# Clustered attention and two feed-forward layers in one kernel: a start with one centroid load and fewer dummy transposes, and another order of moves, masks and splits ahead of the second and third pair of heads

## The chip, the cores and the metric

The kernel runs on one core of a Trainium2 chip as one launch. The metric is device time in microseconds (us). The engines are TensorE (PE; its weight loads have a row of their own, PEld), VectorE (DVE), ScalarE (ACT), GpSimd (POOL) and SyncE (SP), which here only issues DMAs.

## The reference

Inputs: q, k and v of shape (2, 8, 768, 64), 16 centroids for each of 8 heads, and the weights of two feed-forward layers, all float32.

```python
q_assign = argmax(normalise(q) . normalise(centroids))   # k_assign likewise
mask = q_assign[:, :, :, None] == k_assign[:, :, None, :]
scores = where(mask, q k^T / 8, -1e9)
x = softmax(scores) v                                    # as (1536, 512)
x = ((x @ w1) * (x @ w2)) @ w3 @ w_out
out = (sigmoid(x @ w_gate) * (x @ w_val)) @ w_out2
```

## The kernel before, in words

Attention comes first and lasts about 235 us. The 16 heads are worked in 8 pairs (`pr`), a pair's two heads (`e`) lying on partitions 0 to 63 and 64 to 127. A head has three blocks of 256 queries, so there are 48 blocks; block `i` belongs to pair `i // 6` and is its block `at = i % 6`. Every float32 operand is split into a high and a low part in fp32r.

A block's scores are two products for each tile of 128 queries (line 332): KH with QH, and KX with QX. KH holds k's high part in rows 0 to 63 and the mask of the clusters in rows 64 to 79, QH likewise for q; QX holds q's high part and, in rows 64 to 127, q's low part; KX holds k's. The rows are brought together by DMAs within SBUF: `move` (line 62) puts one on SP's queue. `prep_scatter(pr, e)` issues the six moves of a head's operands; `prep_mask(pr, e)` issues the four small moves of its one-hot clusters out of `ohT`, which VectorE turns (line 275) and of which POOL rescales the key half (line 294). For the head (1, 0), `prep_scatter` leaves out the move of q's low part; the kernel does it later by hand.

After the scores come the row maximum (DVE, line 344), the exponential (ACT, line 355), transposes of the exponentials through PE (line 365), their split into `ph` and `pl`, and the products with v (`weighted_v`, lines 406 and 407). The split is done by ACT and DVE, except for the first third of certain blocks (`by_pool`): there ACT copies to the single buffer `pc`, and POOL makes `ph` (line 54) and `pl` (line 59).

A pair's result is joined and normalised while the next pair runs: `join_x` moves, `add_x` (POOL, line 459), `spread` (two DMAs that broadcast the reciprocal sums into `r`, line 454), `norm_x` (POOL, line 463, which needs `r`), and `split_x` (POOL, two instructions).

The order on every engine is written out by hand: the loop over blocks calls these steps one after another, and each engine and each queue takes its instructions in that order. In block 7 (pair 1, `at == 1`) the loop calls `load_v(2)` and `prep_scatter(2, 1)`; in block 9 (`at == 3`) `prep_mask(2, 0)` and `prep_mask(2, 1)`, then `add_x(0)` and `spread(0)`; in block 11 `norm_x(0)` and `split_x(0)` on POOL; in block 12 the splits `ph` and `pl` on POOL, which PE uses in block 13.

Two side chains run along. `prep_split_1_lo` is a generator with three steps for the second pair: k's low part (POOL, line 208), a scaled copy of q (ACT, line 210), and q's low part (POOL, line 212). `f64_steps` turns a weight matrix from words of 64 bits into high and low parts in seven steps; the table `CONVERT` gives the block (pair, `at`) in which each of the later six is called; the last one is the split of the matrix on POOL.

At the start, `warm` issues dummy transposes on PE. The centroids are loaded into both halves of `c2` by two DMAs, then normalised, transposed by PE (line 520) and copied to `cw` (line 533); `prep_sims` multiplies q and k of pair 0 with them (line 241).

After attention the two feed-forward layers run as products of 128 x 512 tiles, with weights split in time by a list of due times. The change does not touch them.

Of the kernel before, what the change touches and what calls it, by code (L numbers as in the profile page):

```python
# [12 lines left out]
ALU = mybir.AluOpType  # L13
# [14 lines left out]
def tile_cluster_attention__then__moe__then__gated_moe(  # L28
# [15 lines left out]
    nc = tc.nc  # L44
# [16 lines left out]
    def move(dst, src):  # L61
        nc.sync.dma_start(dst.bitcast(F32), src.bitcast(F32))
# [70 lines left out]
    def warm(n, name):  # L133

        pt = ps_t.tile([128, 2, 256], F32, tag="t", name=name)
        for i in range(n):
            nc.tensor.transpose(pt[:, 0, 0:128], ident, ident)

    warm(17, "warm0")

    manual = ExitStack()
    manual.enter_context(tc.manual_schedule(engines={mybir.EngineType.PE, mybir.EngineType.DVE, mybir.EngineType.Activation, mybir.EngineType.Pool, mybir.EngineType.SP}))
# [5 lines left out]

    early = core.tile([128, S], F32, tag="xb", name="early", bufs=1)
    c2 = early[:, 0 : 2 * D].rearrange("p (j d) -> p j d", j=2)  # L150
    sq, nrm = early[:, 128:192], early[:, 192:196]
    for j in range(2):
        nc.sync.dma_start(c2[:, j, :], centroids.rearrange("h c d -> (h c) d"))
    cw = cent.tile([128, NP, 2 * C], F32, name="cw")
    nc.gpsimd.memset(cw, 0.0)
    dec = cent.tile([128, C], F32, name="dec")
# [64 lines left out]
    def prep_scatter(pr, e):  # L221
        qh, ql, kh, kl = opnd[pr, "hl"]
        r = slice(64 * e, 64 * e + 64)
        QH, KH, QX, KX = operands(pr, e)
        move(QH[0:64], qh[r])
        move(KH[0:64], kh[r])
        move(QX[0:64], qh[r])
        move(KX[64:128], kh[r])
        move(KX[0:64], kl[r])
        if (pr, e) != (1, 0):  # L230
            move(QX[64:128], ql[r])

    HALF = S // 2

# [43 lines left out]
    def prep_mask(pr, e):  # L278
        ohT = opnd[pr, "oh"]
        QH, KH, _, _ = opnd[pr, e]  # L280
        halves = [slice(HALF * h, HALF * h + HALF) for h in range(2)]
        if pr == 0 and e == 0:
            for h in range(2):
                nc.vector.tensor_scalar(out=KH[64:96, halves[h]], in0=ohT[64 + 32 * h : 96 + 32 * h], scalar1=-1.0, scalar2=BIG, op0=ALU.add, op1=ALU.mult)
                nc.scalar.copy(QH[64:96, halves[h]], ohT[32 * h : 32 * h + 32])
            return
        if pr == 0:
            for h in range(2):
                nc.scalar.activation(KH[64:96, halves[h]], ohT[64 + 32 * h : 96 + 32 * h], AF.Copy, scale=BIG, bias=-BIG)
            nc.scalar.copy(QH[64:96, halves[0]], ohT[0:32])  # L290
            move(QH[64:96, halves[1]], ohT[32:64])
            return
        if e == 0:
            nc.gpsimd.tensor_scalar(out=ohT[64:128], in0=ohT[64:128], scalar1=-1.0, scalar2=BIG, op0=ALU.add, op1=ALU.mult)
        for h in range(2):
            at = 32 * h + C * e
            move(QH[64 : 64 + C, halves[h]], ohT[at : at + C])
            move(KH[64 : 64 + C, halves[h]], ohT[64 + at : 64 + at + C])
# [207 lines left out]

    load_v(0, 0)
    convert(0)
    nc.vector.tensor_tensor(out=sq, in0=c2[:, 0, :], in1=c2[:, 0, :], op=ALU.mult)
    nc.vector.tensor_reduce(out=nrm[:, 0:1], in_=sq, axis=AX.X, op=ALU.add)  # L510
    nc.vector.tensor_scalar(out=nrm[:, 0:1], in0=nrm[:, 0:1], scalar1=1e-30, scalar2=None, op0=ALU.max)
    nc.scalar.activation(nrm[:, 1:2], nrm[:, 0:1], AF.Sqrt)
# [2 lines left out]
    nc.vector.tensor_tensor(out=nrm[:, 2:3], in0=nrm[:, 2:3], in1=nrm[:, 1:2], op=ALU.add)  # L515
    nc.vector.tensor_scalar(out=nrm[:, 2:3], in0=nrm[:, 2:3], scalar1=0.5, scalar2=1e-6, op0=ALU.mult, op1=ALU.add)
    nc.vector.reciprocal(nrm[:, 3:4], nrm[:, 2:3])
    nc.vector.tensor_scalar(out=c2, in0=c2, scalar1=nrm[:, 3:4], scalar2=None, op0=ALU.mult)
    cps = ps_a.tile([128, 128], F32, tag="a", name="cps")
    nc.tensor.transpose(cps, c2.rearrange("p j d -> p (j d)"), ident)  # L520
    warm(5, "warm1")
# [42 lines left out]
    words["av"], words["room"] = both[:, 0:256], both[:, 256:512]  # L564
    CONVERT = {}
    for n, slots in enumerate((
        ((0, 3), (0, 3), (0, 5), (1, 0), (1, 0), (1, 2)),
        ((6, 5), (7, 0), (7, 1), (7, 2), (7, 3), (7, 4)),
    )):
        for slot in slots:  # L570
            CONVERT.setdefault(slot, []).append(n)
    if True:
        for i in range(-2, NB + 2):
            pr, at = divmod(i, 6)
            nxt = pr + 1 if 0 <= i and pr + 1 < NPR else None
            later = nxt + 1 if nxt and nxt + 1 < NPR else None

            scores(2 * i + 3)
            if i == -1:
                warm(11, "warm3")  # L580
            split_hi(i - 1, 2)
            transposes(i, 0)
            if i == NB - 1:
                turn_sums(pr, ps_s.tile([128, 1024], F32, tag="s", name=f"rp{pr}")[:, 0:128])
            maxima(2 * i + 3)
            if i == 0:
                prep_code(0, 1)
                prep_onehot(0, 1)
                prep_turn(0, 1)
                prep_sims(1)  # L590
                prep_sum(1)
            if i == NB - 1:
                store_sums(pr)
            if later and at == 0 and pr:
                load_qk(later)
            if at == 0 and 0 < pr and i < NB:
                join_x(pr - 1, 0)
            if at == 1 and 0 < pr and i < NB:
                join_x(pr - 1, 1)
            if nxt and nxt > 1 and at == 1:  # L600
                load_v(nxt)
                prep_scatter(nxt, 1)
            if nxt and at == 3:
                for e in range(2):
                    if nxt == e == 1:
                        next(split_1_lo, None)
                        move(opnd[1, 0][2][64:128], opnd[1, "hl"][1][0:64])
                        prep_scatter(1, 1)
                    prep_mask(nxt, e)
            split_lo(i - 1, 2)  # L610
            split_hi(i, 0)
            split_lo(i, 0)
            if i == 0:
                prep_v(0, 1)
            if nxt and at == 1:
                prep_argmax(nxt)
            if nxt and at == 2:
                prep_onehot(nxt)
            if 0 < pr and i < NB and at == 5:
                norm_x(pr - 1)  # L620
                split_x(pr - 1)
            if nxt == 1 and at == 2:
                load_v(nxt)
            if 0 < pr and i < NB and at == 3:
                add_x(pr - 1)
                spread(pr - 1, "xb", 1)
            exponentials(2 * i + 3)
            if i == -1:
                next(split_1_lo)
                prep_argmax(0, 1)  # L630
                load_qk(2)
            if 0 <= i < NB and at == 4:
                guard_sums(pr)
            if later and at == 3:
                halves = prep_split(later)
                next(halves)
            if later and at == 4:
                for _ in halves:
                    pass
            weighted_v(i - 1, 0)  # L640
            weighted_v(i - 1, 1)
            if i == 1:
                prep_scatter(1, 0)
            if later and at == 5:
                prep_scatter(later, 0)
            loads = ((6, 4), (7, 1), (7, 3))
            if (pr, at) in loads:
                convert(1 + loads.index((pr, at)))

            similar = later if at == 5 else None  # L650
            if similar:
                prep_sims(similar)
            scores(2 * i + 4)
            turning = 0 <= i < NB - 1 and at == 5
            if turning:
                turn_sums(pr, sps[2 * i + 4][:, S : S + 128])
            if nxt and at == 1:
                prep_code(nxt)
            if 0 < pr < NPR and at == 0:
                prep_v(pr, 1)  # L660
            if nxt and at == 3:
                prep_v(nxt, 0)
            transposes(i, 1)
            split_hi(i, 1)
            weighted_v(i - 1, 2)
            transposes(i, 2)
            if i == NB:
                convert(2)
            take_x(i - 1)
            if i == NB:  # L670
                convert(3)
            if i == 0:
                prep_mask(0, 1)
            if similar:
                prep_sum(similar)
            maxima(2 * i + 4)
            if turning:
                store_sums(pr)
            if nxt and at == 2:
                prep_turn(nxt)  # L680
            if i == NB - 2:
                invert(pr)
            for n in CONVERT.get((pr, at), ()):
                convert(n)
            split_lo(i, 1)
            exponentials(2 * i + 4)
            if 0 <= i < NB - 2 and at == 4:
                invert(pr)
            if i == NB - 2:
                end_move(0)  # L690
            if i == NB:
                end_move(1, FIRST)
                spread(END, "raw", 4)
                end_add(0)
        end_move(1, LAST)
        end_add(1, FIRST)
        end_norm(FIRST)
        end_split(FIRST)
        end_add(1, LAST)
        end_norm(LAST)  # L700
        end_split(LAST)
# [551 lines left out]
```

## Time and profile before

| what | value |
|---|---|
| median of 3 runs | 754.03 us (751.93 to 754.36) |
| the profiled execution | 751.83 us |
| its span, first to last instruction | 749.7 us |
| PE busy | 741.2 us (99%) |
| DVE, ACT, POOL busy | 575.3, 473.2, 415.1 us |
| granted clock of PE, mean | 1.00 |

A row of the timeline reads: start in us from the span's start, duration in us, engine, source line, operation, tile written, tile read, count; in brackets the idle time of the engine just before and what ended it. SPq rows are the issues of DMAs on SP; the duration is that of the issue, not of the transfer. A row with a count above one stands for several instructions in a row.

### The profile page before, as it was taken

The numbers are of one execution on the slowest core, as the hardware profiler recorded it, in microseconds if no ns is written. First come the engines' busy times: TensorE is split into PE (matmuls) and PEld (weight loads), VectorE is DVE, ScalarE is ACT, GpSimd is POOL, SyncE is SP. The second block draws the span as 40 slices with busy tenths as digits, with TensorE's granted clock in tenths as the row PEclk, the third lists the DMA queues.
The fourth block names the chain that finished last, engine by engine and source line by source line (L and its number), as shares of the span: only waits on it lengthen the run. The fifth ranks groups of instructions, "written<-read, shape, count | busy, mean of one in ns | idle before, by whom it ended". The sixth has DMA issues, their size and how long they took to land.

```text
span 749.7 us, 12300 instructions
## 1 busy us (share of the span) xinstructions
PE 741.2 (99%) x4272; PEld 670.9 (89%) x4272; DVE 575.3 (77%) x893; ACT 473.2 (63%) x994; POOL 415.1 (55%) x420
## 2 busy tenths in 40 slices
PE   8999999999999999999999999999999999999998
PEld 6888988999998788888888999999999999999996
DVE  7999999999986677676743386685686968869675
ACT  7988888988985565555532365777757454565630
POOL 4768788878782655424321037775647645375510
PEclk9999999999999999999999999999999999999999
DMA  6687677685542543443430001221303113030004
GB/s 187 168 191 176 170 202 179 166 196 137 144 120 64 159 147 115 143 136 113 142 111 1 1 20 37 86 85 57 114 0 114 56 57 113 28 113 29 30 0 169
DMA packets 29198, 80.14 MB, mean 107 GB/s; under 512 B 5200, under 2 KB 6800, under 8 KB 29136
## 3 DMA queue, kind: packets, MB, share of 16 engines
q1 hardware_dynamic: 29136, 79.35, 36.5%
q8 instruction: 34, 0.56, 0.3%
q14 instruction: 28, 0.23, 0.1%
HBM read 52.49 MB, written 3.19 MB: 74 GB/s over the span
## 4 chain that ended last, share of the span: by engine, by line
PE 88%; DVE 3%; DMA 2%; POOL 2%; ACT 2%; issue 1%; SPq 1%; DVEq 0%; ACTq 0%; POOLq 0%
PE p L67 12%; PE p L66 12%; PE p L65 12%; PE s L332 7%; PE pt L365 7%; PE p_a L66 4%; PE p_a L67 4%; PE p_a L65 4%; PE av L406 4%; PE av L407 4%; PE p_b L65 2%; PE p_b L66 2%; PE p_b L67 2%; PE w34p L65 2%; PE w34p L66 2%; PE w34p L67 2%
## 5 line engine op out<-in xcount | busy, mean ns | idle before, releaser
L344 DVE TENSOR_REDUCE nm<-s 128x1 f32<-128x768 f32 x96 | 90.7, 947 | 8.3 <-PE s L332 7.2
L355 ACT ACTIVATE e<-s,nm 128x768 f32<-128x768 f32 x96 | 88.2, 919 | 11.6 <-DVE nm L344 11.2
L365 PE MATMUL pt<-ident,e 128*128 128x128 f32 x576 | 86.0, 273 | 0.2 <-DVE sm L248 0.2
L406 PE MATMUL av<-ph,vx 128*128 128x256 f32 x288 | 81.1, 309 | 0.1
L67 PE MATMUL p<-x,w 128*128 128x512 f32 (+1 forms) x208 | 80.3, 386 | 0.2 <-POOL w L120 0.2
L66 PE MATMUL p<-x,w 128*128 128x512 f32 (+1 forms) x208 | 80.1, 385 | 0.0
L65 PE MATMUL p<-x,w 128*128 128x512 f32 (+1 forms) x208 | 80.1, 385 | 0.0
L394 DVE TENSOR_TENSOR pl<-pt,ph 128x512 fp32r<-128x512 f32 x113 | 75.7, 682 | 5.0 <-ACT ph L383 3.7
L407 PE MATMUL av<-pl,vx 128*128 128x256 f32 x288 | 74.7, 287 | 0.6 <-DVE pl L394 0.2
L116 POOL TENSOR_TENSOR w_a<-w_f 128x512 uint32<-128x512 uint32 x30 | 32.1, 1070 | 77.2 <-DVE w_f L115 37.1
L383 ACT CAST ph<-pt 128x512 fp32r<-128x512 f32 x113 | 64.7, 590 | 15.0 <-PE pt L365 13.8
L365 PEld LDWEIGHTS pt<-ident,e 128*128 128x128 f32 x576 | 67.7, 141 | 4.5 <-DVE sm L248 0.5
L1132 DVE TENSOR_TENSOR acc<-p,acc 128x512 f32<-128x512 f32 x59 | 40.5, 687 | 29.3 <-PE p L67 29.2
L948 POOL TENSOR_TENSOR wgv_a<-wgv_f 128x512 uint32<-128x512 uint32 x24 | 25.3, 1053 | 66.7 <-DVE wgv_f L947 38.4
L1026 ACT COPY s<-p_a 128x384 f32<-128x384 f32 x72 | 34.5, 479 | 43.2 <-PE p_a L67 42.8
L407 PEld LDWEIGHTS av<-pl,vx 128*128 128x128 f32 x288 | 54.7, 190 | 3.1 <-DVE pl L394 3.0
L67 PE MATMUL p<-wo,u 128*128 128x512 f32 (+1 forms) x146 | 57.3, 393 | 0.0
L66 PE MATMUL p<-wo,u 128*128 128x512 f32 (+1 forms) x146 | 57.1, 391 | 0.0
L332 PE MATMUL s<-KH,QH 80*128 80x512 f32 x192 | 54.6, 366 | 2.4 <-DMA KH<-ohT_None 0.8
L65 PE MATMUL p<-wo,u 128*128 128x512 f32 (+1 forms) x146 | 56.3, 386 | 0.0
L406 PEld LDWEIGHTS av<-ph,vx 128*128 128x128 f32 x288 | 54.5, 189 | 1.8 <-ACT xa L415 0.6
L332 PE MATMUL s<-KX,QX 128*128 128x512 f32 x192 | 49.7, 340 | 0.3 <-DMA QX<-x 0.3
(254 smaller groups left out, 2223.2 us busy)
## 6 DMA issues: line engine op xcount, KB each, us to landing
wgv_f<-in_w_gv_dram SPq DMA_DIRECT2D x24, 512.0 KB, 3.3
wo_f<-in_w_out_dram SPq DMA_DIRECT2D x20, 512.0 KB, 3.2
w_f<-in_w_dram SPq DMA_DIRECT2D x16, 512.0 KB, 3.3
w_f<-in_w3T_dram SPq DMA_DIRECT2D x16, 512.0 KB, 3.3
raw<-in_qkT_dram SPq DMA_DIRECT2D x16, 384.0 KB, 4.5
r<-r_dram SPq DMA_DIRECT2D x16, 192.0 KB, 4.0
xb<-xa SPq DMA_DIRECT2D x15, 192.0 KB, 3.7
out_dram<-acc SPq DMA_DIRECT2D x11, 256.0 KB, 2.0
```

The costliest lines, as they stand in the source:

```text
L65: nc.tensor.matmul(ps, whi, xhi, start=start, stop=False, skip_group_check=more)
L66: nc.tensor.matmul(ps, whi, xlo, start=False, stop=False, skip_group_check=more)
L67: nc.tensor.matmul(ps, wlo, xhi, start=False, stop=stop, skip_group_check=more)
L332: nc.tensor.matmul(sp[:, c], products[n][0], products[n][1][:, c], start=n == 0, stop=n == 1)
L344: nc.vector.tensor_reduce(out=nms[j], in_=sps[j][:, 0:S], axis=AX.X, op=ALU.max, negate=True)
L355: nc.scalar.activation(et, sps.pop(j)[:, 0:S], AF.Exp, bias=nms.pop(j), accum_out=acc_x[pr, "sum"][:, at : at + 1])
L365: nc.tensor.transpose(pt[:, kk, 128 * t : 128 * t + 128], exps[2 * i + t][:, k0 : k0 + 128], ident)
L383: nc.scalar.copy(ph, pt)
L394: nc.vector.tensor_tensor(out=pl, in0=src, in1=ph, op=ALU.subtract)
L406: nc.tensor.matmul(avs[i], w, ph[:, kk, :], start=kt == 0, stop=False)
L407: nc.tensor.matmul(avs[i], w, pl[:, kk, :], start=False, stop=kt == KT - 1)
L1132: nc.vector.tensor_tensor(out=acc[:, t, :], in0=bk, in1=acc[:, t, :], op=ALU.add)
```

## The change

- `warm0` issues 15 dummy transposes in place of 17.
- The centroids are loaded once, into a tile `c1`; the scaling that writes `c2` reads `c1` twice by a broadcast view.
- `prep_scatter` issues all six moves for every head. The third step of `prep_split_1_lo` is called in block 0, ahead of `prep_v(0, 1)`; the separate move of q's low part in block 3 goes.
- `prep_scatter(2, 1)` goes from block 7 to block 9, between `prep_mask(2, 0)` and `prep_mask(2, 1)`.
- The last step of the first weight matrix goes from block (1, 2) to block (1, 1).

```diff
-    warm(17, "warm0")
+    warm(15, "warm0")
...
-    sq, nrm = early[:, 128:192], early[:, 192:196]
-    for j in range(2):
-        nc.sync.dma_start(c2[:, j, :], centroids.rearrange("h c d -> (h c) d"))
+    sq, nrm, c1 = early[:, 128:192], early[:, 192:196], early[:, 200 : 200 + D]
+    nc.sync.dma_start(c1, centroids.rearrange("h c d -> (h c) d"))
...
-        if (pr, e) != (1, 0):
-            move(QX[64:128], ql[r])
+        move(QX[64:128], ql[r])
...
-    nc.vector.tensor_tensor(out=sq, in0=c2[:, 0, :], in1=c2[:, 0, :], op=ALU.mult)
+    nc.vector.tensor_tensor(out=sq, in0=c1, in1=c1, op=ALU.mult)
...
-    nc.vector.tensor_scalar(out=c2, in0=c2, scalar1=nrm[:, 3:4], scalar2=None, op0=ALU.mult)
+    nc.vector.tensor_scalar(out=c2, in0=c1.unsqueeze(1).broadcast_to([128, 2, D]), scalar1=nrm[:, 3:4], scalar2=None, op0=ALU.mult)
...
-        ((0, 3), (0, 3), (0, 5), (1, 0), (1, 0), (1, 2)),
+        ((0, 3), (0, 3), (0, 5), (1, 0), (1, 0), (1, 1)),
...
                 load_v(nxt)
-                prep_scatter(nxt, 1)
+                if nxt > 2:
+                    prep_scatter(nxt, 1)
             if nxt and at == 3:
                 for e in range(2):
                     if nxt == e == 1:
-                        next(split_1_lo, None)
-                        move(opnd[1, 0][2][64:128], opnd[1, "hl"][1][0:64])
                         prep_scatter(1, 1)
                     prep_mask(nxt, e)
+                    if nxt == 2 and e == 0:
+                        prep_scatter(2, 1)
...
             if i == 0:
+                next(split_1_lo, None)
                 prep_v(0, 1)
```

## Rows read from the trace of the kernel before

**Rows 1.** The page's busy times: us, share of the span, instructions

```profile
PE 741.2 (99%) x4272; PEld 670.9 (89%) x4272; DVE 575.3 (77%) x893; ACT 473.2 (63%) x994; POOL 415.1 (55%) x420
```

**Rows 2.** PE's waits: line, releaser, us in total, times, longest

```profile
PE s L332 <- DMA KH<-ohT_None: 0.8, 1, 0.8
...
PE s L332 <- DVE KH L284: 0.6, 1, 0.6
PE s L332 <- DMA QX<-x: 0.3, 1, 0.3
```

**Rows 3.** Timeline of the start, all engines

```profile
0.74 0.86 SPq L153 DMA_DIRECT2D early<-in_centroids_dram  x2
...
4.38 0.29 DVE L518 TENSOR_SCALAR early<-early 128x128 f32<-128x128 f32 x1
...
5.64 0.46 DVE L533 COPY cw<-cps 64x64 f32<-64x64 f32 x2 [0.97 <-PE cps L520]
...
6.41 0.83 ACT L529 CAST KH<-raw 64x768 fp32r<-64x768 f32 x1 [0.37 <-DMA raw<-in_qkT_dram]
```

**Rows 4.** Stretches, dummies' loads: length, PEld busy (count), granted clock, DMA share, GB/s

```profile
1.51:4.99 3.48, 3.48 (x17) 1.00 0.70 202
7.19:10.23 3.04, 3.04 (x28) 1.00 0.76 299
```

**Rows 5.** Timeline of POOL and PE's loads, blocks 0 to 3

```profile
21.45 1.02 POOL L59 TENSOR_TENSOR vx<-vraw,vx 128x384 fp32r<-128x384 f32 x1
24.02 0.62 POOL L54 TENSOR_SCALAR ph<-pc 128x512 fp32r<-128x512 f32 x1 [1.54 <-ACT pc L380]
26.41 0.19 PEld L407 LDWEIGHTS av<-pl,vx 128*128 128x128 f32 x1
31.52 1.85 POOL L212 TENSOR_TENSOR x<-q,x 128x768 fp32r<-128x768 f32 x1
```

**Rows 6.** Timeline of blocks 7 to 10, the third pair's moves

```profile
55.52 0.46 SPq L62 DMA_DIRECT2D QH<-hi  x1
...
56.20 0.62 POOL L54 TENSOR_SCALAR ph<-pc 128x512 fp32r<-128x512 f32 x1 [1.86 <-PE s L332]
...
58.18 0.57 DVE L275 STREAM_TRANSPOSE ohT_None<-oh 128x384 f32<-128x384 f32 x1
...
60.39 0.83 SPq L62 DMA_DIRECT2D QH<-ohT_None  x1
...
62.85 0.58 SPq L62 DMA_DIRECT2D KH<-ohT_None  x1
...
64.94 0.59 PE L332 MATMUL s<-KH,QH 80*128 80x512 f32 x2 [0.79 <-DMA KH<-ohT_None]
...
66.06 1.18 SPq L454 DMA_DIRECT2D r<-r_dram  x2
```

**Rows 7.** One stretch, the weight tile on POOL: length, POOL busy (count), clock, DMA

```profile
58.50:60.60 2.10, 1.90 (x2) 1.00 0.98 222
```

**Rows 8.** Timeline of blocks 11 to 13, POOL and PE's loads

```profile
70.45 1.85 POOL L463 TENSOR_TENSOR xa<-xa,r 128x768 f32<-128x768 f32 x1 [1.41 <-DMA r<-r_dram]
...
75.82 1.27 POOL L59 TENSOR_TENSOR pl<-pc,ph 128x512 fp32r<-128x512 f32 x1
...
77.61 0.19 PEld L407 LDWEIGHTS av<-pl,vx 128*128 128x128 f32 x1
```

**Rows 9.** The tile r over the whole span: from issue to landing

```profile
DMA to landing us min/median/max: 3.7/4.0/4.8
```

**Rows 10.** Timeline of SP's queue, second pair's masks and moves

```profile
30.80 0.54 SPq L62 DMA_DIRECT2D QH<-ohT_None  x1
...
33.40 0.50 SPq L62 DMA_DIRECT2D QX<-x  x1
...
38.99 0.87 SPq L62 DMA_DIRECT2D QH<-ohT_None  x1
...
42.19 0.53 SPq L62 DMA_DIRECT2D QH<-hi  x1
```

## The prediction

> **What bounds the kernel now.** I read the page's busy times first, then TensorE's waits, then the timeline of the places where it waits. TensorE (PE) is busy for 741.2 of 749.7 us [rows 1]: time can only come out of its few idle stretches, and any new one is added in full. Its list of waits names three that the change touches [rows 2]: 0.8 us for a mask move into KH, 0.6 us for the first mask (DVE, line 284), 0.3 us for a move into QX. In the timeline the reader then looks, for each, at what stands just ahead of the late instruction on its own queue, and who is next in that queue.
>
> **Start: one centroid load, two dummies fewer.** The two centroid loads take 0.86 us of issue on SP, 0.43 us each [rows 3]; with one gone everything SP issues afterwards, the q and k of the first pair first, is issued 0.43 us sooner. ScalarE's KH waits for k at 6.41 [rows 3], so that should become 5.98. The normalised centroids are ready at 4.38 + 0.29 = 4.67 (then 4.24), but VectorE idles 0.97 us until 5.64 for their transpose [rows 3], which stands behind the 17 dummies; their weight loads fill 3.48 us up to 4.99 [rows 4], 0.205 us each. Two fewer let the transpose start 0.41 us sooner, at 4.58, still after the centroids. Similarities need both: they move by 0.41 us, and the chain on VectorE behind them leads to the mask for which PE waits [rows 2]. The broadcast operand in the scaling of the centroids I cost at nothing: the same 128x128 output, whose 0.29 us would hide in the 0.34 us between 4.24 and 4.58. I take -0.4; the bounds are -0.43 (the whole issue) and 0 (k lands no sooner because earlier transfers do not speed up its bytes).
>
> The loads of the dummies went from 0.205 us to 3.04 / 28 = 0.109 us each between the two stretches, the 1.2 and the 2.4 GHz level by their ratio of 1.9, although the granted clock in the record reads 1.00 in both [rows 4]; nearly everything that PE did until then was transposes. The Trainium skill, page "TensorE: Matmul & The Clock Gate", section "Part 4: PE-mode transpose", says that a transpose does not count as PE work in the same way and that full rate does not engage for it. By that rule dropping two dummies could not touch the clock, and the sum stays at -0.4; by the rows, dummies do raise it, so that fewer of them could raise it later. That is a rival below.
>
> **Second pair: q's low part.** POOL's 1.85 us subtraction at line 212 moves from 31.52 into block 0, ahead of the v split that ended at 21.45 + 1.02 = 22.47 [rows 5]. Behind that split POOL idled 1.54 us until 24.02 for `pc` [rows 5]; 1.85 us more is 0.3 us too many, and the low product of block 1 comes 0.3 us late. PE loads exactly that at 26.41 [rows 5], so I price +0.3 (0 to +0.35). In return the last QX move of this head no longer stands behind the subtraction: it joins the other five at block 1, many us before its use, and the 0.3 us wait goes [rows 2]. SP issues as many moves as before; the second head's six move up by one issue, and nobody waits for them. Net 0, from -0.3 to +0.35.
>
> **Weight split a block sooner.** Its two instructions, 1.90 us, now lie between 58.5 and 60.6 on POOL [rows 7], between `ohT_None`, ready at 58.18 + 0.57 = 58.75 [rows 6], and line 294, which two of the four mask moves need. One block sooner it falls into POOL's 1.86 us of idle time ahead of 56.20 [rows 6]. So nearly all of it is covered: at worst 0.1 us sticks out ahead of block 8. Nothing, by itself; it lets line 294 run at 58.75.
>
> **Third pair: masks first.** Now SP issues six moves of the second head from 55.52, then, from 60.39, eight mask moves, then at 66.06 the two loads of the reciprocal sums `r` [rows 6]. PE needs the first head's masks at 64.15 and gets them at 64.94, from the fourth mask move, issued at 62.85 [rows 6]: 0.79 us lost. After the change the order is four masks, six moves, four masks, `r`. The masks can start at 58.75; four of them took 2.6 us in the second pair (30.80 to 33.40) [rows 10], so the fourth is issued about 60.7, 2.1 us sooner. The 0.79 us goes.
>
> What is late next is `r`. The same 14 issues stand ahead of it, but the train starts at 58.75 and not at 55.52; SP has nothing to do in between. The train took 66.06 - 55.52 = 10.54 us [rows 6]; so `r` is issued at 69.3, 3.2 us later. The second pair has the new order already, with one issue more: 30.80 to 42.19 [rows 10], 11.39 us for 15, or 10.6 for 14. Now POOL is the queue that matters. Its line 463 starts at 70.45, after idling 1.41 us for `r`, and behind it stand, in order, the two splits of x and block 12's `ph` and `pl`; `pl` ends at 75.82 + 1.27 = 77.09 and PE loads it at 77.61 [rows 8]. The slack is 0.52 us. Shifted by 3.2 us, `pl` ends at 80.3 and PE's load comes at 80.35: 2.7 us later than now, with the 0.79 us already counted in (without that gain PE would be there at 76.8 and stand for 3.5 us). ScalarE's next copy into the one `pc` buffer waits along with it, as PE does, and adds nothing. No later wait of PE gives the time back [rows 2].
>
> From both sides: if all 14 issues ran at the 0.65 us of four masks, the train would be 9.1 us, `r` 1.8 us late and PE +1.3; with `r` landing after the longest 4.8 us instead of the 3.8 us that its second issue had here (about 66.65 to 70.45) [rows 8, 9], +3.7. I take +2.6, close to the train of rows 6 with a small deduction for masks that start on an empty queue.
>
> **Sum.** -0.4 + 0 + 2.6 = +2.2 us. The profiled run took 751.83 us (749.7 of span and 2.1 around it), 2.2 us less than the median of 754.03; so the median would go to 756.2, +0.29%. A measurement of this kernel can tell about 0.3% (2.26 us) from no change: the forecast lies at that edge, just inside.
>
> **Rivals.**
> A later `r` (slower): place, POOL line 463. For it: `r` has landed up to 4.8 us after issue, and after the change it follows six large moves more closely. Against: the median is 4.0 [rows 9]. At +3.7 for the third pair, 757.3; it decides from the point where `r` lands 0.1 us later than I take it.
> A faster train: 14 issues at 0.65 us, +1.3 for the pair, +0.9 in all, 754.9. For it: large moves go out at 0.6 us each until some are outstanding. Against: the six from 55.52 to 60.39 took 0.81 us each [rows 6].
> The aim alone (faster): the 0.79 and 0.4 us are won and no product is late, -1.2 us, 752.8. It needs `r` within 0.5 us of its present landing; the fixed order of SP and POOL speaks against it. Allowing for noise, half of it would be read as faster.
> The clock rises later (slower): with 15 dummies the second level might come only behind the 28 dummies ahead of the first scores. Price at most 28 x (0.205 - 0.109) = 2.7 us, on top of 2.2: 758.9. Against: PE stays without a gap until about 5.1 as now, since transpose and dummies follow at once.
>
> **Chances.** Forecast 0.56 (0.30 within 0.3%, 0.26 above it, since its spread of about 0.7 us straddles the bound); later `r` 0.15; faster train 0.13; aim alone 0.12 (half faster, half same); clock 0.04. Hence faster 0.06, same 0.30 + 0.13 + 0.06 = 0.49, slower 0.26 + 0.15 + 0.04 = 0.45. The range runs from the aim alone to a later `r` with the slower train, 752.8 to 757.8; the forecast's own is 755.4 to 757.0.
>
> **What would show it.** Right: the first similarities begin near 5.75; the wait on KH<-ohT_None is gone and the fourth mask move issued near 60.3; `r` issued near 68.8; POOL line 463 behind an idle time of some 4.5 us; PE with a new wait of about 3.4 us on POOL's `pl` at block 13, none after it. Wrong: `r` issued before 67, or PE passing block 13 without a wait (the aim alone); dummies at 0.2 us still in the second stretch (clock); a wait of PE later than 90 us would mean that SP's lag went on into the fourth pair, which I do not count.

## The result and the profile after

The changed kernel takes 757.46 us (median of 6 runs, 756.68 to 758.92) against 753.41 us (6 runs, 751.93 to 754.36): a ratio of 1.0057, 95% interval 1.0042 to 1.0072. It is slower by about 4 us. The forecast was 756.2, with a range of 752.8 to 757.8 that holds the measured time; the direction came out, the size was about half, and the place of the loss was another.

TensorE's waits in the changed kernel, as in [rows 2] (line numbers are up to two lower: line 332 is now 330):

```profile
PE av L404 <- ACT xa L413: 4.7, 1, 4.7
...
PE s L330 <- DVE KH L282: 0.2, 1, 0.2
```

The waits on `KH<-ohT_None` and on `QX<-x` are gone, as forecast. In their place stands one of 4.7 us, and it is on ScalarE, not on POOL. The timeline of blocks 8 to 10, all engines, answers to [rows 6]:

```profile
58.04 0.54 SPq L62 DMA_DIRECT2D QH<-ohT_None  x1
...
60.32 0.57 SPq L62 DMA_DIRECT2D KH<-ohT_None  x1
...
60.94 0.59 SPq L62 DMA_DIRECT2D QH<-hi  x1
...
62.27 0.53 SPq L62 DMA_DIRECT2D QX<-hi  x1
...
65.52 0.84 ACT L192 ACTIVATE hi<-raw 128x768 fp32r<-128x768 f32 x1 [5.04 <-DMA QX<-hi]
...
66.73 0.38 ACT L413 COPY xa<-av 128x256 f32<-128x256 f32 x1
...
67.16 0.49 PE L404 MATMUL av<-ph,vx 128*128 128x256 f32 x1 [4.69 <-ACT xa L413]
...
68.57 1.18 SPq L452 DMA_DIRECT2D r<-r_dram  x2
```

In block 9 ScalarE starts the split of the fourth pair (`prep_split(3)`, line 192) and writes a new `hi`. The tag `hi` has two buffers, and the buffer that comes round held the third pair's high part of q. Two of the six moves that went to block 9 read it, QH at 60.94 and QX at 62.27. ScalarE therefore stands for 5.04 us until QX has landed; behind it in its queue stand the copy of `av` (line 413) and the exponentials, and PE needs that copy. In the kernel before, the six moves had been issued from 55.52 [rows 6], and ScalarE wrote the same `hi` without a wait, by its timeline:

```profile
61.14 0.85 ACT L193 ACTIVATE hi<-raw 128x768 fp32r<-128x768 f32 x1
```

The wait costs a second time. Stretches of the changed kernel: length, then busy time and count for PE, PEld, DVE, ACT and POOL, then granted clock, DMA share and GB/s:

```profile
58.00:62.40 4.40, 4.34 (x32) 3.78 (x31) 3.51 (x6) 2.48 (x6) 3.88 (x4) 1.00 0.14 37
62.40:67.10 4.70, 0.06 (x1) 0.00 (x0) 0.24 (x1) 1.58 (x4) 0.00 (x0) 1.00 0.98 212
67.10:68.00 0.90, 0.84 (x4) 0.84 (x5) 0.90 (x2) 0.90 (x4) 0.00 (x0) 0.60 0.76 178
68.00:69.00 1.00, 1.00 (x7) 1.00 (x6) 0.91 (x2) 1.00 (x3) 0.00 (x0) 0.50 0.15 40
```

After 4.7 us of nothing on PE the granted clock is 0.50, the 1.2 GHz level, until about 70.7. From the late product at 67.16 to the product at 70.81 PE needs 3.65 us for eight products with v, four products of the scores and four transposes; at a granted clock of 1.00 the same work takes 2.11 us (67.89 to 70.00 in the experiment that keeps PE busy, below): 1.5 us lost.

A ruler that does not contain the start is the time between the turns of the one-hot (DVE, line 275 of before) of the third and fourth pair: 27.80 us before (58.18 [rows 6] to 85.98), 33.22 us after (57.44 to 90.66). DVE's timelines, one row of before and two of after:

```profile
85.98 0.57 DVE L275 STREAM_TRANSPOSE ohT_None<-oh 128x384 f32<-128x384 f32 x1
...
57.44 0.57 DVE L273 STREAM_TRANSPOSE ohT_None<-oh 128x384 f32<-128x384 f32 x1
...
90.66 0.57 DVE L273 STREAM_TRANSPOSE ohT_None<-oh 128x384 f32<-128x384 f32 x1
```

The difference of 5.4 us is 4.69 for the new wait, less 0.79 for the old one, plus 1.5 for the clock. The start gives 0.64 us back in this execution (the first one-hot is turned at 10.07, before at 10.71); the two profiled executions differ by 4.85 us (756.68 and 751.83).

### The profile page after: what moved, and what is told of

It reads as the page before. It is cut to its first block, busy times and chain, and to the rows that moved or that the text cites. A ratio compares the mean times of both kernels' runs of the same rounds, so it can differ in the third digit from the quotient of the medians.

```text
span 754.7 us, 12290 instructions
## 1 busy us (share of the span) xinstructions
PE 742.6 (98%) x4270; PEld 672.2 (89%) x4270; DVE 575.6 (76%) x893; ACT 473.5 (63%) x994; POOL 414.7 (55%) x420
## 4 chain that ended last, share of the span: by engine, by line
PE 92%; DVE 2%; ACT 2%; DMA 1%; issue 1%; POOL 1%; SPq 0%; DVEq 0%; ACTq 0%; POOLq 0%
PE p L67 13%; PE p L66 13%; PE p L65 13%; PE s L330 8%; PE pt L363 7%; PE p_a L66 4%; PE p_a L67 4%; PE p_a L65 4%; PE av L404 4%; PE av L405 4%; PE p_b L65 2%; PE p_b L66 2%; PE p_b L67 2%; PE w34p L67 2%; PE w34p L66 2%; PE w34p L65 2%
```

## The experiments

Ratios are against the kernel before, with their 95% intervals; "ruler" is the time just defined, from the one profiled execution of each kernel.

| kernel | ratio | ruler, us |
|---|---|---|
| before; once more | 1 | 27.80; 28.26 |
| the change; once more | 1.0057 (1.0042 to 1.0072) | 33.22; 34.58 |
| change, own buffers | 1.0079 (1.0066 to 1.0093) | 33.72 |
| change, six moves back in block 7 | 0.9988 (0.9978 to 0.9998) | 28.67 |
| before, the six moves moved, no more | 1.0102 (1.0088 to 1.0116) | 35.70 |
| own buffers and `r` ahead of the six moves | 1.0059 (1.0046 to 1.0072) | 26.91 |
| six moves ahead of the join | 0.9995 (0.9986 to 1.0005) | 29.19 |
| start alone | 0.9988 (0.9978 to 0.9998) | 27.40 |
| change, PE kept busy | 1.0045 (1.0033 to 1.0057) | 32.23 |
| q's low part and weight split alone | 0.9985 (0.9976 to 0.9993) | 27.51 |

**Own buffers for the fourth pair.** `spare` is a part of x that, by the order in the code, gets its own values in block 35 (`split_x(4)`) at the earliest.

```diff
-            hi = core.tile(..., tag="hi", ..., bufs=2)
-            lo = core.tile(..., tag="lo", ..., bufs=2)
+            if pr == 3:
+                hi, lo = spare(w, 0), spare(w, 1)
+            else:
+                ... as before
```

> The change whole, but the fourth pair's high and low parts lie in the spare half of x instead of the rotating buffers that the third pair's moves read. Theory A (the loss is ScalarE: its first write of the fourth pair's high part waits for the moved six moves that still read that buffer, and PE waits 4.7 us for what stands behind it): that wait of 5.0 us on ScalarE and the 4.7 us on PE in block 10 go, and the low clock after it. Theory B (the forecast: r is issued late, POOL's normalisation and block 12's low product are late): then it shows now, because nothing else holds PE: r issued near 68.6, POOL idle some 5 us before its normalisation, the low product ends near 80, PE stands some 3.8 us at block 13, about +2.3 us against the kernel before in all. If B is wrong and only A held PE, the time is about 1.5 us below the kernel before.

ScalarE's wait is gone and so is PE's in block 10: theory A is shown. And theory B shows behind it. POOL and PE, timeline (line numbers are three higher than in the changed kernel):

```profile
74.29 1.85 POOL L464 TENSOR_TENSOR xa<-xa,r 128x768 f32<-128x768 f32 x1 [5.57 <-DMA r<-r_dram]
...
79.89 0.58 PE L407 MATMUL av<-ph,vx 128*128 128x256 f32 x1 [3.22 <-POOL ph L54]
81.23 0.58 PE L408 MATMUL av<-pl,vx 128*128 128x256 f32 x1 [0.76 <-POOL pl L59]
```

That is the wait of the forecast: POOL idle for `r`, PE standing 4.0 us at block 13 where 3.4 to 3.8 were said. But the kernel lost 6.0 us, not 2.3: after this wait too the granted clock fell, by the stretches of the same kernel (columns as above):

```profile
78.00:80.00 2.00, 0.11 (x1) 0.11 (x1) 1.32 (x2) 0.00 (x0) 1.92 (x3) 0.78 0.94 323
80.00:82.00 2.00, 1.24 (x4) 0.94 (x5) 0.00 (x0) 0.79 (x2) 1.92 (x3) 0.50 0.70 209
82.00:84.00 2.00, 2.00 (x10) 1.81 (x9) 0.00 (x0) 0.69 (x2) 1.92 (x3) 0.50 0.48 100
84.00:86.00 2.00, 2.00 (x11) 2.00 (x10) 1.00 (x2) 0.59 (x1) 1.65 (x2) 0.52 0.97 297
86.00:88.00 2.00, 2.00 (x18) 1.92 (x17) 1.40 (x2) 1.89 (x5) 0.00 (x0) 1.00 1.03 215
```

From 79.89 to 86.27 PE needs 6.38 us, 0.76 of them the second wait, for what took 2.99 us before (77.53 to 80.52): the clock costs 2.6 us here. Together, 4.0 + 2.6 - 0.79 is the 5.9 us by which the ruler is longer. In the change, ScalarE's wait came first and hid this one: POOL's normalisation starts at 73.37 there, with no idle time ahead of it.

**`r` ahead of the six moves as well.**

```diff
                     if nxt == 2 and e == 0:
+                        add_x(0)
+                        spread(0, "xb", 1)
                         prep_scatter(2, 1)
...
-            if 0 < pr and i < NB and at == 3:
+            if 1 < pr and i < NB and at == 3:
                 add_x(pr - 1)
                 spread(pr - 1, "xb", 1)
```

> As the first of this group (own buffers for the fourth pair), and the first pair's add and its two loads of r stand ahead of the six moves. Theory A and B together: neither ScalarE nor POOL holds PE, all gains stay: the start's 0.65, the second pair's 0.1, the 0.79 of the masks, about 1.5 us below the kernel before. If r was never what limits (B wrong), the time is that of the first kernel of this group.

In the third pair all is as hoped: the ruler reads 26.91, the shortest of all. The time is that of the change nevertheless. PE's wait has moved into the fourth pair; SP and PE, timeline:

```profile
83.33 0.46 SPq L62 DMA_DIRECT2D xa<-xa  x1
...
90.21 0.87 SPq L62 DMA_DIRECT2D QH<-ohT_None  x1
...
92.64 0.58 SPq L62 DMA_DIRECT2D KH<-ohT_None  x1
...
94.68 0.59 PE L333 MATMUL s<-KH,QH 80*128 80x512 f32 x2 [3.66 <-DMA KH<-ohT_None]
```

The fourth pair's one-hot was turned at 85.03 + 0.57 = 85.60, and SP came to its first mask at 90.21. In the kernel before, the same two issues stood at

```profile
79.71 0.46 SPq L62 DMA_DIRECT2D xa<-xa  x1
...
86.57 0.55 SPq L62 DMA_DIRECT2D QH<-ohT_None  x1
```

with the one-hot turned at 85.98 + 0.57 = 86.55. SP is 3.6 us later at both: the third pair's issues had started at 58.71 in place of 55.52, and that lag was handed on through its queue. This wait is followed by a low clock as well (0.50 from 96 to 98 us). The next ruler, from the fourth to the fifth pair, is 32.20 us (85.03 to 117.23) against 26.95 before. Three places thus wait for the same late queue, one behind the other, and freeing one shows the next.

**The move alone.**

```diff
                 load_v(nxt)
-                prep_scatter(nxt, 1)
+                if nxt > 2:
+                    prep_scatter(nxt, 1)
...
                     prep_mask(nxt, e)
+                    if nxt == 2 and e == 0:
+                        prep_scatter(2, 1)
```

> The kernel before with only the six moves of the third pair's second head moved between the two groups of masks; the weight split stays in block (1, 2). POOL's rescaling of the masks then comes at 60.6 and holds SP up, so that the six moves go out from about 63 and the second QX-high move lands near 68. Theory A: ScalarE waits until about 68 (7 us), PE about as long, minus the 0.79 us, plus about 1.4 us for the lower clock: about +7 us. Theory B: r is issued near 71, 5 us late, POOL's low product of block 12 ends near 82: about +4.5 us.

+7.6 us, close to theory A's 7. ScalarE idles 6.40 us ahead of its `hi`, PE 6.05 us, by the timeline of both in this kernel:

```profile
67.42 0.84 ACT L193 ACTIVATE hi<-raw 128x768 fp32r<-128x768 f32 x1 [6.40 <-issue]
...
69.06 0.58 PE L406 MATMUL av<-ph,vx 128*128 128x256 f32 x1 [6.05 <-ACT xa L415]
```

The trace names no releaser for ScalarE here ("issue"); the QX move was issued at 64.10, 3.3 us ahead of ScalarE's start, as in the change (62.27 and 65.52), and that is how the wait is read. The parts of the expectation were not as near as its sum: the wait of PE was 6 us in place of 7, and the clock cost about 2.6 us in place of 1.4 (the ruler is 7.9 us longer, less 6.05 for the wait, plus 0.79 for the old one).

**The change without the move.** The edit of the last diff, undone in the changed kernel.

> The change, but with the six moves of the third pair's second head back in block 7 (before the masks); start, q's low part and weight split as in the change. Both theories lay the whole loss on this move: no wait of ScalarE or POOL is left, the 0.79 us wait of PE on the masks is back, and the time is about 0.7 us below the kernel before (the start's 0.65 us, 0.1 us from the second pair). A rival that the start or the POOL reorder costs something would give the kernel before's time or more.

Measured 0.9988, about -0.9 us. The loss of the change lies in this one move. The mask wait is back, with 1.3 us in this execution. ScalarE, too, waits a little for the moves here, which the expectation had ruled out:

```profile
60.98 0.85 ACT L192 ACTIVATE hi<-raw 128x768 fp32r<-128x768 f32 x1 [0.50 <-DMA KX<-hi]
```

In the kernel with the start alone this wait is 0.32 us. The place in block 7 had little slack against ScalarE to begin with.

**PE kept busy through the wait.**

```diff
             scores(2 * i + 3)
+            if i == 10:
+                for _ in range(36):
+                    nc.tensor.transpose(sps[23][:, S : S + 128], ident, ident)
```

> The change with 36 dummy transposes on PE in block 10, behind the scores and ahead of the block's own transposes, that is in the time in which PE stands waiting for ScalarE. Their results are read by nobody. If the 3.6 us at half the granted clock after the wait are part of the loss, they go and the time is about 1.4 us below the change; the wait of ScalarE of 5.0 us on the moves stays. If the clock's share is hidden by ScalarE's backlog behind the wait, the time is that of the change.

PE's timeline in this kernel, around the wait:

```profile
62.44 4.09 PE L579 MATMUL s<-ident 128*128 128x128 f32 x36
66.37 0.60 PE L363 MATMUL pt<-ident,e 128*128 128x128 f32 x4
67.89 0.38 PE L404 MATMUL av<-ph,vx 128*128 128x256 f32 x1 [0.93 <-ACT xa L413]
```

Its stretches, with the columns as above:

```profile
62.00:68.00 6.00, 5.07 (x45) 4.79 (x43) 0.48 (x2) 1.75 (x4) 0.77 (x1) 1.00 0.86 186
68.00:69.00 1.00, 1.00 (x9) 1.00 (x10) 1.00 (x2) 1.00 (x3) 0.00 (x0) 1.00 0.55 135
```

ScalarE waits as before (5.20 us), the clock stays at 1.00, and the ruler is 1.0 us shorter than the change's, not 1.4: 0.16 us are ScalarE's longer wait, 0.16 us a new wait of PE for POOL at 72.46, and the rest is not accounted for. In the times the ratio falls from 1.0057 to 1.0045, but the intervals overlap: the trace shows the clock's share, the times only agree with it.

**Six moves ahead of the join.** In block 7 SP stands idle because one join move waits for another to land; here the six moves go first.

```diff
+            if nxt == 2 and at == 1:
+                prep_scatter(nxt, 1)
             if at == 1 and 0 < pr and i < NB:
                 join_x(pr - 1, 1)
...
-                    if nxt == 2 and e == 0:
-                        prep_scatter(2, 1)
```

> The change, but the third pair's six moves for its second head stand in block 7 ahead of the first pair's join moves (one of which holds SP until 53.4, waiting for another to land). Theory C (SP's queue is what the masks, ScalarE's buffer and r compete for; what must not happen is that it stands idle ahead of the masks): the six moves go out from about 51.5 to 56, the masks at 58.0 as soon as the one-hot is turned, r no later than 65; none of PE's waits of blocks 9 to 20 is left, about 1.9 us below the kernel before, 1.0 below the variant with the six moves back in block 7. Rival: the join move and the load of v, now some 2 to 3 us later, hold POOL's add and its split of v in block 9, and PE gets a wait of 0.5 to 1 us on POOL in block 10 or 11: no gain over that variant.

The rival held: no gain that can be measured. The moves go out from 48.2, yet POOL waits for the join and PE for the masks and for POOL (1.04 and 0.93 us). POOL's timeline in this kernel:

```profile
62.64 1.83 POOL L457 TENSOR_TENSOR xa<-xa,xb 128x768 f32<-128x768 f32 x1 [4.14 <-DMA xa<-xa]
```

That join move was issued at 54.05 and took 8.4 us to land. The DMA share of its stretches (second from the right) fits this:

```profile
50.00:52.00 2.00, 2.00 (x19) 1.91 (x17) 1.97 (x4) 1.68 (x4) 1.84 (x2) 1.00 1.08 243
56.00:58.00 2.00, 2.00 (x17) 1.89 (x16) 2.00 (x4) 1.46 (x4) 1.60 (x2) 1.00 1.06 219
```

From 48 to 60 us the 16 DMA engines are full (share 0.98 to 1.08 in every stretch of 2 us). With so many transfers in these 12 us, another order seems only to choose which one is late; that no order does better is not shown.

**The two remaining parts alone.** The first kernel is the one before with the start of the change, the second has q's low part and the weight split.

> The kernel before with only the start changed: 15 dummies, one centroid load. Forecast: the first masked scores 0.4 us sooner, -0.4 us. By the traces so far the centroids land between 2.42 and 2.69 with one load as with two, and the first masked scores at 11.6 to 12.2 against 12.0 to 12.2: a gain of 0 to 0.6 that changes from one execution to the next; -0.2 in the mean, which a measurement may not tell from nothing.

> The kernel before with only q's low part put back (its subtraction in block 0) and the weight split a block sooner. Forecast: +0.3 and -0.3 in the second pair, nothing from the weight split by itself: 0. The traces show the wait of 0.3 on QX gone and no new wait of 0.3 in block 2; the masks of the third pair still stand behind the six moves, so that wait stays between 0.8 and 1.3: -0.1 to -0.3 in all.

Both are faster by about 1 us, 0.9988 and 0.9985, and so is the change without the move, which has both. That is more than was expected of either, and the parts do not add up; all three intervals end just below 1, and where the gains come from is open. What the start gives differs from one execution to the next: over 8 traces with one load the first one-hot is turned at 9.81 to 10.73, mean 10.25; over 4 with two loads at 10.29 to 10.71, mean 10.43. The third pair's masks' wait is in neither trace; at the same product PE stands 0.20 and 0.48 us for ScalarE. In the second kernel the second pair's wait on QX is gone, and one of 0.29 us on a mask move into KH stands in the second pair instead.

**Both kernels once more.**

> The kernel before, unchanged, one execution more. If the 0.79 us wait on the third pair's masks belongs to the kernel, it is there again; the kernels with only the start or only q's low part changed had none in their execution, so I expect it to change between 0 and 1.3 us with the landing of the moves, and with it what there was to win.

> The change, unchanged, one execution more. The loss should be the same each time, as it hangs on the order: ScalarE waits 4.5 to 5.5 us for the moves in block 9, PE 4.2 to 5.2 us behind it, then 3 to 4 us at half the granted clock; 32.5 to 33.5 us between the one-hot turns of the third and the fourth pair, against 27.4 to 27.8 without the move.

They took 754.04 and 756.75 us, one execution each. PE's waits in the kernel before, in its second execution:

```profile
PE s L332 <- DMA KH<-ohT_None: 1.3, 1, 1.3
...
PE s L332 <- DMA QX<-x: 0.6, 1, 0.6
```

The masks' wait is 1.3 us here. Over the five traces in which the six moves stand in block 7 behind the join (the kernel before twice, the change without the move, the start alone, and q's low part with the weight split alone), the masks' wait was 0.79, 1.3, 1.3, 0 and 0 us. The change's loss stays where it was in its second execution, by the timeline of ScalarE and PE:

```profile
65.40 0.84 ACT L192 ACTIVATE hi<-raw 128x768 fp32r<-128x768 f32 x1 [5.16 <-DMA QX<-hi]
...
67.05 0.58 PE L404 MATMUL av<-ph,vx 128*128 128x256 f32 x1 [4.83 <-ACT xa L413]
```

Its low clock lasts longer than expected, until about 73 us; hence its ruler of 34.58, over the 32.5 to 33.5 that were said. Its stretches:

```profile
72.00:73.00 1.00, 1.00 (x6) 1.00 (x5) 0.73 (x2) 0.86 (x2) 1.00 (x1) 0.50 0.98 246
73.00:74.00 1.00, 1.00 (x9) 0.89 (x8) 0.18 (x1) 0.89 (x3) 1.00 (x2) 0.94 1.02 215
```

## Why the prediction was right or wrong

- **Third pair, "the 0.79 us goes": right.** The fourth mask move is issued at 60.32 (forecast 60.3), the wait is gone. But what there was to win was one execution's number, between 0 and 1.3 us in others.
- **"What is late next is `r`": the step that failed.** The prediction followed who stands behind the moved six moves on SP, and did not ask what they read. A late reader keeps its source buffer, and the next writer of the buffer, ScalarE in block 9, stands ahead of `r` in time. The experiment with own buffers shows that this is the cause; the one that makes the move alone gives its size when the masks are held up besides.
- **`r` itself: right in mechanism, hidden in the change.** `r` went out at 68.57 (forecast 68.8). With ScalarE freed, POOL idled 5.57 us for it and PE stood 4.0 us at block 13. That is more than the forecast's 4.5 and 3.4: `r` took 4.5 us to land there, where the sum took 3.8, which is the rival of a later `r`. In the change PE reached block 13 too late to notice it, so a sign that the prediction had put down for being wrong, PE passing block 13 without a wait, came true for a reason that it did not have.
- **"A wait of PE later than 90 us ... which I do not count": wrong to leave out.** With the third pair freed it came at 94.68, 3.66 us; in the change itself no mask was late there (the one-hot was turned only at 91.23, and SP was free for it by then), and PE's one wait of over 0.3 us behind 90 us is 0.52 us at 97.17, for ScalarE.
- **The clock: mis-sized as nothing.** "Any new one is added in full" priced a wait at its length. Here it costs more: 1.5 us on top in the change, 2.6 with own buffers, and the second execution of the change shows that one and the same wait can be followed by a short or a long stretch at the low clock. In the rivals the clock stood only for the start.
- **Start, -0.4: mis-sized.** Forecast: centroids 0.43 us sooner. They landed at 2.42 to 2.69 us with one load, 2.42 to 2.47 with two, so not sooner at all; PE then waits for them (0.34 us ahead of line 518 in the change), not for its dummies. The first similarities began at 6.15 in the change as in the kernel before, where 5.75 was said, and at 5.70 in its second execution. The rival of a clock that rises later did not come: the 28 dummies' loads fill 3.04 us in the change as before. The sum of both edits is about -0.2 us in the mean of the traces.
- **Second pair, 0: right within 0.3.** The wait on QX is gone; POOL's `ph` of block 1 starts at 23.48, 0.54 us sooner than [rows 5], where the gain of the start, 0.65 in this execution, would have it: 0.1 us late in place of 0.3, and no wait of PE. What there was to win varied here too: with the old order the wait on QX was 0.28, 0.53 and 0.61 us in three traces and absent in a fourth.
- **Weight split, nothing by itself: the traces fit it.** It fits POOL's gap, as said. It does not decide the masks' wait: the start alone, with the split in its old place, has none, and the change without the move, with the split a block sooner, has 1.3 us.

The forecast's +2.2 thus came near the +4 by missing a wait of 4.7 us, putting one of 3.5 us that did not show in its place, and leaving out the clock. The direction follows from what the prediction saw, that the move makes later users of SP's queue late; that the time lies inside its range is luck.

## What to carry to other kernels

When a transfer is moved later, follow two lists: who is queued behind it, and who will next write what it reads; a buffer that rotates makes a late reader stop an engine that has nothing to do with it. The queue of this kernel had no slack to give: the idle time that the new order put in front of it came out somewhere, and removing the first wait showed the next one. A wait that lets the clock fall costs more than its length. So a wait of 0.8 us in one trace is worth fixing only if the order that fixes it leaves no hole, and only if the wait is there in other executions too. Of the changed kernel, all but that move can be kept: without it the kernel is 0.12% faster than before (0.02 to 0.22%).

## What was not expected of the hardware

- After 4.7 to 4.8 us without work on PE the granted clock read 0.50 for some 3.4 us in one execution of the change (about 67.3 to 70.7) and some 6.8 us in another (about 66.3 to 73.1); after the gaps of 0.79 and 1.3 us on the masks it stayed at 1.00. With 36 transposes in the gap whose results nobody reads it stayed at 1.00.
- Six moves of 192 KB within SBUF, with small mask moves among them, kept all 16 DMA engines busy at 212 GB/s (share 0.98, the change from 62.40 to 67.10). In the full stretches of the kernel with the six moves ahead of the join, one such move took 8.4 us to land; in the kernel before, the medians of such moves are 2.9 to 4.8 us, by the tile that they write.
